# A list of doubtful rows cut in two blocks, expert blocks between and beside them, and one branch at the end of the tail

## The chip, the core and the metric

The kernel runs on one core of one Trainium2 chip. TensorE (PE) does the matrix products, VectorE (DVE) and ScalarE (ACT) the elementwise work and the copies out of PSUM, GpSimd (POOL) issues the indirect transfers (gathers and scatters of rows by index), SyncE (SP) the plain ones. The metric is the device time of one execution in microseconds (us), the median of several runs.

## The reference, cut to what matters

```python
x = _attn_ref(x, w_r, w_i, b_r, b_i).reshape(B * S, D)   # rfft, mix, shrink, irfft: 8 x 3072 rows of 256
h = x @ w_in                                             # first feed-forward, 2048 wide
x = (s * np.maximum(h, 0.0) ** 2 + b) @ w_out
logits = x @ w_gate                                      # second one: 8 experts of 1024, top 1
e = np.argmax(logits, axis=1)
gate = softmax(logits)[arange, e]
# a row is kept while its expert has had fewer than 768 rows before it, in order; out is 0 for the others
out[i] = gate[i] * (np.maximum(x[i] @ w1[e[i]], 0.0) @ w2[e[i]])
```

## The kernel before, in words

The order of the instructions is written out by hand (`manual_schedule`); each engine takes its own in that order. The main part (to about 1447 us) goes through the eight batches, 64 steps (`s_unit`) each. It finds for every row by a bound whether the row can go to an expert that isn't full. The first 1024 rows are computed exactly; after them one expert is full, and only rows whose choice stays open are put on a list in DRAM (`list`), at the place counted in `base` (one `decide_items` for each batch, whose last eight pieces are POOL scatters, L877).

`tail` does the rest:

- `decide_items` of the last batch, among `blocks[0]` and `blocks[1]`. A block (`block_steps`) is 128 rows of the full expert: two transposes (L1413), a copy `yT` by ACT, 32 matmuls `ph` (L1423), 16 matmuls `po` (L1433), the gated copy `o` by ACT and a scatter to `out` by POOL (L1438). There are `blocks[0]` to `blocks[5]`; each begins with transposes that wait for nothing but its rows and ends with matmuls into one PSUM tile.
- `whole_list`: a branch (L888) whose body writes the whole list anew where a lane had more than eight listed rows.
- `ids`: reads 512 entries of the list (an SP transfer `ci`, then eight small DVE operations), `load` gathers their rows (`ga`, two POOL gathers for 256 rows).
- `blocks[2]`, then `e2_steps` twice: for 256 listed rows each the exact logits and the exact output of the first feed-forward (`x_in`, L923; `x_mm`, L934; `x_out`, L949; `x_lg`, L957).
- `xroute_items` (softmax, ranks, tables `T`; DVE chains with four small matmul groups) among the ten steps of `blocks[3]`.
- `e2_more`: a branch (L1555) whose body takes more than two blocks of listed rows and then repeats the six blocks.
- `final_tables` (six pieces `a, d, e, d1, f, g`) among the twenty steps of `blocks[4]` and `blocks[5]`. The last piece `g` makes the indices of the other experts' rows and issues every load of theirs: gathers `yr`, `gg`, `nr`, `ng` and ten weight transfers of 1 MiB (`w`, `wb`, two `wq`, `wa`; each expert is a `w1`, L1348, and a `w2`, L1349).
- `item(0)`, nested with `item(1)`, ... (L1445): one block of another expert inside a branch each. `small(0)`, nested with `small(1)`, ... (L1463): up to three experts of at most 32 rows each, inside a branch.

A branch not taken is a jump over its body on every engine; behind it each engine makes up for the semaphore steps of the body, and POOL does so with `INC_SWDGE_SEM`.

Of the kernel before, what the change touches and what calls it, by code (L numbers as in the profile page):

```python
# [18 lines left out]
S = 3072  # L19
# [105 lines left out]
S_FROM = 27  # L125
S_TO = 62
# [22 lines left out]
class Kern:  # L149
# [625 lines left out]
    def route_consts(self, pp):  # L775
# [29 lines left out]
        self.cmax = zero("cmax", [1])  # L805
# [75 lines left out]
    def whole_list(self):  # L881

        nc, V = self.nc, self.nc.vector
        ovf = nc.values_load(self.ovf[0:1, 0:1], min_val=0, max_val=128)
# [355 lines left out]
    def final_tables(self, p2):  # L1240
# [30 lines left out]
        def e():  # L1271
# [12 lines left out]
            V.tensor_copy(out=t("ints", [2], I32), in_=endb[:, :, E - 1])  # L1284
# [158 lines left out]
    def item(self, n):  # L1443

        with self.tc.If(self.nblk > n):  # L1445
            if n > 1:
                self.load_item(n)
                self.rows(self.yr[n % 2], self.idy[:, n:n + 1])
                self.gate(n)
            for f in self.block_steps(self.wx[n % 2], self.yr[n % 2], self.gg[n % 2], self.ids[:, n:n + 1], "o2"):  # L1450
                f()
            if n + 1 < NI:
                self.item(n + 1)

# [4 lines left out]
    def small(self, g):  # L1459

        nc, pq = self.nc, self.pq
        P = 32 * NQ
        with self.tc.If(self.nsml > NQ * g):  # L1463
            if g:
                self.small_load(g, *range(NQ))
                self.rows(self.nr[:P], self.nids[:, 2, g:g + 1])
                self.gather(self.ng[:P], self.gd, self.nids[:, 0, g:g + 1])
            pt = pq.tile([128, 512], F32, tag="py", name="pt4", bufs=4)
            for h in range(2):
                nc.tensor.transpose(pt[:, h * P:(h + 1) * P], self.nr[:P, h * 128:(h + 1) * 128], self.ident[:P, :P])  # L1470
            yT = self.pb.tile([128, 2, P], F32, tag="yT", name="yT", bufs=2)
            nc.scalar.copy(out=yT.rearrange("p h c -> p (h c)"), in_=pt[:, :2 * P])
            hs, hT, os = {}, {}, {}

            def first(n):

                ps = pq.tile([128, 512], F32, tag="h", name="ph4", bufs=3)
                for h in range(2):
                    for j in range(4):
                        nc.tensor.matmul(ps[32 * j:32 * j + 32, :C], yT[:, h, 32 * n:32 * n + 32],  # L1480
                                         self.wq[n][0][:, h, C * j:C * (j + 1)], start=(h == 0), stop=(h == 1),
                                         skip_group_check=True)
                hs[n] = self.pb.tile([128, 2, 128], F32, tag="yT", name="hs", bufs=2)
                nc.scalar.activation(out=hs[n].rearrange("p c f -> p (c f)"), in_=ps[:, :C], func=AF.Relu)

            def turn(n):
                pt = pq.tile([128, 512], F32, tag="py", name="pt5", bufs=4)
                for c in range(2):
                    nc.tensor.transpose(pt[:, c * 128:(c + 1) * 128], hs[n][:, c], self.ident)
                hT[n] = self.pb.tile([128, 2, 4, 32], F32, tag="xq", name="hT", bufs=4)  # L1490
                nc.vector.tensor_copy(out=hT[n].rearrange("p c j t -> p (c j t)"), in_=pt[:, :C])

            def second(n):
                po = pq.tile([128, 512], F32, tag="py", name="po4", bufs=4)
                for c in range(2):
                    for j in range(4):
                        nc.tensor.matmul(po[32 * j:32 * j + 32, :C], hT[n][:, c, j], self.wq[n][1][:, 2 * j + c],
                                         start=(c == 0), stop=(c == 1), skip_group_check=True)
                os[n] = self.pb.tile([128, C], F32, tag=("eh", "el", "y")[n], name="os", bufs=(2, 2, 1)[n])
                nc.scalar.copy(out=os[n], in_=po[:, :C])  # L1500
            for n in range(NQ + 3):
                for f, k in ((first, 0), (turn, 1), (second, 3)):
                    if 0 <= n - k < NQ:
                        f(n - k)
            pr = pq.tile([128, 512], F32, tag="py", name="pr4", bufs=4)
            for n in range(NQ):
                nc.tensor.matmul(pr[32 * n:32 * n + 32, :C], self.sel, os[n], start=True, stop=True,
                                 skip_group_check=True)
            o = self.pb.tile([128, C], F32, tag="o4", name="o4", bufs=1)
            nc.scalar.activation(out=o[:P], in_=pr[:P, :C], func=AF.Copy, scale=self.ng[:P])  # L1510
            nc.gpsimd.indirect_dma_start(  # L1511
                out=self.out, out_offset=bass.IndirectOffsetOnAxis(ap=self.nids[:, 1, g:g + 1], axis=0),
                in_=o[:P], in_offset=None, bounds_check=self.B * S - 1, oob_is_err=False)
            if g + 1 < NS:
                self.small(g + 1)
# [29 lines left out]

    def e2_more(self, p2, again):
# [3 lines left out]
        bi, rem, blk = self.rt("e2i", [1], I32), self.rt("e2r", [1]), self.rt("e2b", [2])  # L1550
# [3 lines left out]
        n = nc.values_load(bi[0:1, 0:1], min_val=0, max_val=(self.B * S - XT) // TD)  # L1554
# [22 lines left out]
    def tail(self, es, e1, e3, p2):  # L1577
# [23 lines left out]
        tables, regs = self.final_tables(p2b)  # L1601
# [11 lines left out]
        def load(k):  # L1613
            x[k] = self.x_load(self.gbuf[k % 2], x["c"][3][:, 2 * k:2 * k + 2])
# [5 lines left out]
        self.lg_fin(B - 1, 7)  # L1620
        blocks = [block(j) for j in range(NJ)]
# [27 lines left out]
        among(blocks[4] + blocks[5], tables)  # L1649
        regs()  # L1650
        self.item(0)
        self.small(0)


    def run(self):
# [5 lines left out]
        with ExitStack() as es, tc.manual_schedule():  # L1661
# [89 lines left out]
            for b in range(B):  # L1751
# [15 lines left out]
                if b == B - 1:  # L1767
# [15 lines left out]
                    slot.setdefault(S_TO, []).extend(lambda j=j: self.full_rows(j) for j in range(NJ))  # L1783
                    self.yf = [p2.tile([128, C], F32, tag=f"yf{j}", name=f"yf{j}") for j in range(NJ)]
# [27 lines left out]
                for k in range(64):  # L1812
# [9 lines left out]
                    while fin and fin[0][0] <= 64 * b + k:  # L1822
                        _, fb, fi = fin.pop(0)
                        self.lg_fin(fb, fi)
                        if fi == 7 and fb > 1:
                            todo += self.decide_items(fb)
                    if todo:
# [53 lines left out]
```

## Time and profile before

| | us |
|---|---|
| median of 3 runs | 1633.86 |
| the three runs | 1641.65, 1633.6, 1633.86 |
| profiled execution, its own time | 1641.85 |
| its span, first to last instruction | 1640.1 |
| mean granted TensorE clock, share of full speed | 0.964 |

Times in the profile count from the first instruction of the span. "Idle before, releaser" tells how long an engine had nothing to do before an instruction and which instruction's end let it go on; "issue" is a wait that no recorded event explains. A jump has no busy time: it is seen as COMPARE_BRANCH on the sequencer (PEldq for PE). The clock column is the share of 2.4 GHz that was granted; 0.5 is 1.2 GHz.

### The profile page before, as it was taken

How to read it: one execution, taken by the hardware profiler on the slowest of the kernel's cores; microseconds unless marked ns; L12 is line 12 of the kernel's file. 1: busy time of each engine (PE TensorE's matmuls, PEld its weight loads, DVE VectorE, ACT ScalarE, POOL GpSimd, SP SyncE). 2: the span in 40 equal slices, each digit the busy share in tenths (PEclk: the TensorE clock that was granted, in tenths of full speed). 3: DMA queues.
4: the chain of work that ended last, by engine and by line, in shares of the span. 5: the costliest groups of instructions: out<-in, count | busy, mean ns of one | idle time of the engine just before them, and what ended most of it. 6: DMA issues, size and time to landing. Idle time of an engine off the chain costs nothing. (4 is left out here: it accounts for less than half of the span.)

```text
span 1640.1 us, 26008 instructions
## 1 busy us (share of the span) xinstructions
PE 1474.6 (90%) x9469; PEld 1223.8 (75%) x9469; DVE 957.3 (58%) x2057; ACT 814.6 (50%) x1252; POOL 267.8 (16%) x235
## 2 busy tenths in 40 slices
PE   8987899989998799999999999999999978988865
PEld 5876688777876578768877887787688768977753
DVE  2956467446555667656765775576567675623410
ACT  2335633754334564575467447645754665623311
POOL 0534100100000130030013002100300161231020
PEclk9998999999999899999999999999999989989978
DMA  8625644644434454464456446544644356510034
GB/s 258 219 91 187 170 141 145 188 128 128 144 111 139 113 145 138 144 165 139 130 148 169 144 125 171 152 137 144 165 142 128 97 136 204 170 40 17 14 113 174
DMA packets 273572, 230.03 MB, mean 140 GB/s; under 512 B 120045, under 2 KB 228335, under 8 KB 273424
## 3 DMA queue, kind: packets, MB, share of 16 engines
q1 hardware_dynamic: 255664, 200.13, 42.5%
q10 hardware_dynamic: 13936, 25.21, 4.1%
q0 software_dynamic: 3824, 2.82, 0.7%
q8 instruction: 80, 1.31, 0.4%
q14 instruction: 68, 0.56, 0.1%
HBM read 114.18 MB, written 114.09 MB: 139 GB/s over the span
## 5 line engine op out<-in xcount | busy, mean ns | idle before, releaser
L723 PE MATMUL ph<-ah,win 128*128 128x384 f32 (+1 forms) x2048 | 490.7, 368 | 7.4 <-ACT r L728 6.7
L728 ACT ACTIVATE r<-ph 128x768 bf16<-128x768 f32 (+1 forms) x512 | 396.0, 784 | 162.4 <-PE ph L723 118.8
L729 DVE TENSOR_TENSOR qb<-r 128x768 bf16<-128x768 bf16 (+1 forms) x512 | 300.8, 589 | 286.3 <-ACT r L728 258.7
L723 PEld LDWEIGHTS ph<-ah,win 128*128 128x128 f32 x2048 | 347.5, 194 | 77.6 <-issue 40.4
L333 PE MATMUL pmx<-wm,l 128*128 128x256 f32 x1196 | 297.1, 387 | 17.4 <-DVE kb L343 9.6
L396 POOL TENSOR_TENSOR asq<-ah 128x768 bf16<-128x768 f32 x64 | 96.2, 1504 | 1049.0 <-ACT ah L392 977.0
L333 PEld LDWEIGHTS pmx<-wm,l 128*128 128x128 f32 x1196 | 221.1, 191 | 54.7 <-DVE kb L343 16.0
L390 PEld LDWEIGHTS pi<-f1t,u 96*128 96x128 f32 x1024 | 131.3, 199 | 17.1 <-issue 8.4
L390 PE MATMUL pi<-f1t,u 96*128 96x96 f32 x1024 | 135.9, 284 | 6.1 <-DVE l L260 4.3
L224 PE MATMUL pz<-x,f 96*96 96x512 f32 x240 | 125.3, 606 | 3.7 <-DMA f<-c_f 3.7
L259 ACT COPY l<-pf 128x512 f32<-128x512 f32 x84 | 49.2, 586 | 144.5 <-PE pf L251 144.1
L371 ACT COPY v<-pi 128x512 f32<-128x512 f32 x96 | 56.3, 587 | 125.2 <-PE pi L369 125.2
L369 PE MATMUL pi<-t,e 128*128 128x256 f32 x384 | 99.5, 382 | 5.1 <-DVE t L328 5.1
L251 PEld LDWEIGHTS pf<-d,zp 128*128 128x128 f32 x672 | 89.5, 195 | 13.0 <-issue 7.9
L251 PE MATMUL pf<-d,zp 128*128 128x128 f32 x672 | 90.6, 279 | 8.2 <-DMA zp<-zd 8.2
L406 DVE STREAM_TRANSPOSE at<-pi 128x384 f32<-128x384 f32 x128 | 74.1, 579 | 34.1 <-ACT ah L392 25.5
L392 ACT CAST ah<-pi 128x384 fp32r<-128x384 f32 x128 | 61.1, 479 | 59.1 <-PE pi L390 58.9
L369 PEld LDWEIGHTS pi<-t,e 128*128 128x128 f32 x384 | 72.6, 191 | 17.5 <-DVE t L328 6.9
L232 ACT COPY z<-pz 96x512 f32<-96x512 f32 x120 | 69.8, 581 | 25.0 <-PE pz L224 18.3
L328 DVE TENSOR_TENSOR t<-t,cl 128x512 f32<-128x512 f32 x96 | 73.1, 762 | 3.3
L877 POOL DMA_INDIRECT list<-c,x x64 | 65.7, 1027 | 45.1 <-DVE c L873 29.0
L759 ACT COPY ls<-lg 128x384 f32<-128x384 f32 (+1 forms) x64 | 52.8, 825 | 24.0 <-PE lg L746 13.6
(395 smaller groups left out, 1818.6 us busy)
## 6 DMA issues: line engine op xcount, KB each, us to landing
zd<-z SPq DMA_DIRECT2D x128, 192.0 KB
zp<-zd SPq DMA_DIRECT2D x96, 256.0 KB
vd<-v ACTq DMA_DIRECT2D x96, 256.0 KB
u<-vd SPq DMA_DIRECT2D x64, 384.0 KB
ad<-at SPq DMA_DIRECT2D x256, 96.0 KB
out<-zero SPq DMA_DIRECT2D x96, 256.0 KB
x<-x SPq DMA_DIRECT2D x120, 192.0 KB
sd<-stage SPq DMA_DIRECT2D x32, 256.0 KB
```

The source lines that it names most:

```text
L224: nc.tensor.matmul(o, self.f1, xs.rearrange("p a c -> p (a c)"), start=True, stop=True)
L232: nc.scalar.copy(out=z.rearrange("p a c -> p (a c)"), in_=o)
L251: nc.tensor.matmul(pv[:, h, :, gi * 64:gi * 64 + 64], zp[:, gi, h * 128:(h + 1) * 128], self.d[:, 2 * p + gi, :].rearrange("p (t m) -> p t ...
L328: nc.vector.tensor_tensor(out=t, in0=t, in1=cl, op=ALU.subtract)
L333: self.nc.tensor.matmul(o, part(h), w[:, h], start=start and h == 0, stop=stop and h == 1, skip_group_check=True)
L369: nc.tensor.matmul(ps[:, gi * C:(gi + 1) * C], self.e[:, 2 * p + gi], t[:, gi * C:(gi + 1) * C], start=True, stop=True)
L390: nc.tensor.matmul(ps[:, :TC].rearrange("p (a n) -> p a n", n=4)[:, :, n], u[:, n, h::2], self.f1t, start=True, stop=True)
L396: nc.gpsimd.tensor_tensor(out=self.asq[b, i], in0=af, in1=af, op=ALU.mult)
L406: nc.vector.transpose(out=self.ar[:, :, :, h], in_=self.at.pop((b, i, h))[:, :TC].rearrange("p (g c) -> p g c", c=32))
L723: nc.tensor.matmul(ps[:, j, :n], self.win[:, k, f], ah[:, k, t0:], start=(k == 0), stop=(k == 1))
L728: nc.scalar.activation(out=r, in_=ps[:, :, :n], func=AF.Relu)
L729: nc.vector.tensor_tensor(out=q, in0=r, in1=r, op=ALU.mult)
```

## The change: what it does

1. **First list block early.** At step 60 of the last batch `first_block` reads the first 256 list entries, copies `base` to `early` and gathers their rows. In the tail the first `e2` block (`part(0)`) takes the place of `blocks[0]` and `blocks[1]` as the work among which the last batch is decided.
2. **`whole_list`** is also taken where `early` is under 256, and its body ends with `redo`: `part(0)` again with a fresh read and gather.
3. **Between the list blocks**: `ids`, one gather of 256 rows, then `blocks[0]` and `blocks[1]`, then the second `e2` block. `line` writes two blocks so that the second one's transposes stand before the first one's `po` matmuls.
4. **Beside the ranks**: `xroute_items` among the twenty steps of `blocks[2]` and `blocks[3]`. The number for the second branch is computed (`e2_number`) and read into registers (`e2_count`) before them.
5. **Beside the tables**: all six pieces stand among the first ten steps of `line(blocks[4:])`, so `g` comes after the `po` matmuls of `blocks[4]`; ten steps follow it.
6. **One branch**: the steps of items 0 and 1 (in `line`) and of the first group of small experts (`small_do(0)`) always run. One number, `more`, is read at the end; the branch holds `item(2)` and `small(1)` with their own nests.

The diff (unchanged lines of `small` that only lost a level are left out):

```diff
@@ whole_list
+    def whole_list(self, redo):
+        V.tensor_scalar(out=self.early, in0=self.early, scalar1=float(TD), scalar2=None, op0=ALU.is_lt)
+        V.tensor_tensor(out=self.ovf, in0=self.ovf, in1=self.early, op=ALU.add)
+        ovf = nc.values_load(self.ovf[0:1, 0:1], min_val=0, max_val=129)
...
                 for n in range(N2):
                     self.to_list(n, x, c)
+            redo()
@@ final_tables
+            more = t("more", [2])
+            for k, n in enumerate((2, NQ)):
+                V.tensor_scalar(out=more[:, k:k + 1], in0=endb[:, k, E - 1:E], scalar1=float(-n), scalar2=0.0, op0=ALU.add, op1=ALU.max)
+            V.tensor_tensor(out=v["ints"][:, 2:3], in0=more[:, 0:1], in1=more[:, 1:2], op=ALU.add)
...
         def r():
             ints = v["ints"]
-            self.nblk = nc.values_load(ints[0:1, 0:1], min_val=0, max_val=NI)
-            self.nsml = nc.values_load(ints[0:1, 1:2], min_val=0, max_val=E - 1)
+            more = nc.values_load(ints[0:1, 2:3], min_val=0, max_val=NI + E)
+            with self.tc.If(more > 0):
+                self.nblk = nc.values_load(ints[0:1, 0:1], min_val=0, max_val=NI)
+                self.nsml = nc.values_load(ints[0:1, 1:2], min_val=0, max_val=E - 1)
+                self.item(2)
+                self.small(1)
@@ e2
+    def e2_count(self):
+        self.nlist = self.nc.values_load(self.bi[0:1, 0:1], min_val=0, max_val=(self.B * S - XT) // TD)
+
+    def first_block(self):
+        c = self.e2_ids(2, self.list[0:TD], None, self.base)
+        self.nc.vector.tensor_copy(out=self.early, in_=self.base)
+        self.first_rows = self.x_load(self.gbuf[0], c[3])
@@ tail
-        blocks = [block(j) for j in range(NJ)]
-        among(blocks[0] + blocks[1], self.decide_items(B - 1))
-        self.whole_list()
+        def part(k, rows):
+            return self.e2_steps(lambda: rows, lg, 2 * k, self.yx[XT + TD * k:XT + TD * (k + 1)])
+
+        def redo():
+            c = self.e2_ids(2, self.list[0:TD], None, self.base)
+            for f in part(0, self.x_load(self.gbuf[0], c[3])):
+                f()
+
+        def line(blocks):
+            it = [f for f in blocks[0][:5]]
+            for n, b in enumerate(blocks):
+                nx = blocks[n + 1] if n + 1 < len(blocks) else []
+                it += nx[:1] + b[5:] + nx[1:5]
+            return it
+        blocks = [block(j) for j in range(NJ)]
+        among(part(0, self.first_rows), self.decide_items(B - 1))
+        self.whole_list(redo)
         ids()
-        for k in range(min(SB, 2)):
-            load(k)
-        lg = self.rt("e2g", [2 * SB, E])
-        for f in blocks[2]:
+        rows = self.x_load(self.gbuf[1], x["c"][3][:, 2:4])
+        self.e2_number()
+        for f in line(blocks[0:2]) + part(1, rows):
             f()
-        for k in range(SB):
-            st = self.e2_steps(lambda k=k: x[k], lg, 2 * k, self.yx[XT + TD * k:XT + TD * (k + 1)])
-            st.pop(0)()
-            if k + 2 < SB:
-                load(k + 2)
-            for f in st:
-                f()
+        self.e2_count()
...
-        among(blocks[3], side)
+        among(line(blocks[2:4]), side)
...
-        among(blocks[4] + blocks[5], tables)
-        regs()
-        self.item(0)
-        self.small(0)
+        it = line(blocks[4:])
+        among(it[:10], tables)
+        for f in it[10:]:
+            f()
+        for f in line([self.item_steps(n) for n in range(2)]):
+            f()
+        self.small_do(0)
+        further()
@@ run
+                    slot.setdefault(LIST_AT, []).append(self.first_block)
```

## Rows read from the trace of the kernel before

**Rows 1.** The page: span, and TensorE's clock in 40 slices of it.

```profile
span 1640.1 us, 26008 instructions
...
PEclk9998999999999899999999999999999989989978
```

**Rows 2.** Stretches of the tail: length; busy PE, PEld, DVE, ACT, POOL; clock; DMA, GB/s.

```profile
1449.30:1457.00 7.70, 6.22 (x28) 5.83 (x29) 3.58 (x12) 0.97 (x2) 4.73 (x5) 0.56 0.32 102
...
1515.95:1545.99 30.04, 28.17 (x233) 24.65 (x231) 12.29 (x20) 10.30 (x18) 0.00 (x0) 1.00 0.03 10
1563.99:1569.60 5.61, 5.09 (x23) 4.69 (x23) 1.12 (x8) 0.92 (x2) 0.00 (x0) 0.50 0.01 3
...
1617.10:1629.30 12.20, 9.74 (x110) 4.49 (x110) 1.27 (x3) 3.05 (x8) 0.94 (x1) 0.85 0.06 21
1629.30:1640.10 10.80, 0.00 (x0) 0.00 (x0) 0.00 (x0) 0.00 (x0) 0.00 (x0) 0.58 0.03 7
```

**Rows 3.** Waits of PE from 1440 us on: who waited for whom.

```profile
PE pt L1413 <- DMA yr<-zd,idi: 7.9, 1, 7.9
PE pt L1470 <- ACTq L1445: 6.4, 1, 6.4
PE pt L1413 <- DVE sc L1283: 5.8, 1, 5.8
PE ph L1423 <- ACT yT L1415: 3.9, 7, 0.7
PE ptb L1117 <- DVE ol L1110: 2.4, 2, 2.0
PE pt L923 <- DMA ga<-ad,cw: 2.1, 2, 1.3
PE ph L1423 <- issue: 2.1, 1, 2.1
...
PE pt L1413 <- PEq L888: 1.3, 1, 1.3
```

**Rows 4.** PE's jump at each branch line: duration ns min/median/max, first, last start.

```profile
L888 PEldq COMPARE_BRANCH  x1: 247/247/247, 1467.5 to 1467.5; - x1
...
L1555 PEldq COMPARE_BRANCH  x1: 3914/3914/3914, 1559.5 to 1559.5; - x1
...
L1445 PEldq COMPARE_BRANCH  x1: 6357/6357/6357, 1608.0 to 1608.0; - x1
...
L1463 PEldq COMPARE_BRANCH  x3: 65/197/3648, 1614.8 to 1630.8; - x3
```

**Rows 5.** Timeline of PE: the end of the last batch, one block.

```profile
1448.65 0.64 PE L767 MATMUL plt<-ident,ls 128*96 128x128 f32 x4 [0.91 <-ACT ls L759]
...
1603.46 3.84 PE L1423 MATMUL ph<-yT,wb 128*128 128x128 f32 x32 [0.66 <-ACT yT L1415]
1607.14 3.62 PE L1433 MATMUL po<-wb,h 128*128 128x256 f32 x16
```

**Rows 6.** Timeline of SP: the weight transfers' issue, first and last.

```profile
1585.73 0.40 SPq L1348 DMA_DIRECT2D w<-moe_w  x1
...
1602.05 5.59 SPq L1348 DMA_DIRECT2D wa<-moe_w  x1
```

**Rows 7.** Stretches of the weight transfers, columns as in rows 2.

```profile
1585.73:1617.60 31.87, 17.45 (x102) 15.40 (x102) 0.00 (x0) 3.97 (x8) 8.02 (x8) 0.78 1.00 347
...
1617.60:1620.30 2.70, 2.24 (x22) 0.97 (x24) 0.00 (x0) 0.40 (x2) 0.00 (x0) 0.50 0.14 49
```

**Rows 8.** Timeline of all engines: the third small expert, the last scatter.

```profile
1621.68 1.07 PE L1480 MATMUL ph<-wa,yT 128*32 128x256 f32 x16
...
1628.32 0.94 POOL L1511 DMA_INDIRECT out<-o,idn  x1 [15.45 <-ACTq L1463]
```

**Rows 9.** Timeline of SP and POOL: reading the list, gathering its rows.

```profile
1477.59 0.38 SPq L1523 DMA_DIRECT2D ci<-list  x1
...
1480.83 1.04 POOL L1395 DMA_INDIRECT ga<-ad,cw  x1 [6.37 <-DVE e2p L1611]
```

More of the change, by code (lines that the diff above doesn't have):

```diff
@@ L125 @@
 S_FROM = 27
+LIST_AT = 60
 S_TO = 62
@@ L1283, in e @@
             V.tensor_tensor(out=sc[:, 0:2], in0=endb, in1=sc[:, 2:4], op=ALU.subtract)
-            V.tensor_copy(out=t("ints", [2], I32), in_=endb[:, :, E - 1])
+            V.tensor_copy(out=t("ints", [3], I32)[:, 0:2], in_=endb[:, :, E - 1])
+            more = t("more", [2])
+            for k, n in enumerate((2, NQ)):
+                V.tensor_scalar(out=more[:, k:k + 1], in0=endb[:, k, E - 1:E], scalar1=float(-n), scalar2=0.0, op0=ALU.add, op1=ALU.max)
+            V.tensor_tensor(out=v["ints"][:, 2:3], in0=more[:, 0:1], in1=more[:, 1:2], op=ALU.add)
         def f():
@@ L1445, in item @@
         with self.tc.If(self.nblk > n):
[L1446 to L1450, printed above, removed]
+            self.load_item(n)
+            self.rows(self.yr[n % 2], self.idy[:, n:n + 1])
+            self.gate(n)
+            for f in self.item_steps(n):
                 f()
@@ L1453, in item, with item_steps @@
                 self.item(n + 1)
+    def item_steps(self, n):
+        return self.block_steps(self.wx[n % 2], self.yr[n % 2], self.gg[n % 2], self.ids[:, n:n + 1], "o2")
     def small_load(self, g, *qs):
@@ L1459, in small, with small_do @@
     def small(self, g):
+        P = 32 * NQ
+        with self.tc.If(self.nsml > NQ * g):
+            self.small_load(g, *range(NQ))
+            self.rows(self.nr[:P], self.nids[:, 2, g:g + 1])
+            self.gather(self.ng[:P], self.gd, self.nids[:, 0, g:g + 1])
+            self.small_do(g)
+            if g + 1 < NS:
+                self.small(g + 1)
+    def small_do(self, g):
         nc, pq = self.nc, self.pq
         P = 32 * NQ
[L1463 to L1468, printed above, removed]
-            for h in range(2):
[L1470 to L1515, printed above, removed]
@@ new lines, in small_do, with first @@
+        pt = pq.tile([128, 512], F32, tag="py", name="pt4", bufs=4)
+        for h in range(2):
+            nc.tensor.transpose(pt[:, h * P:(h + 1) * P], self.nr[:P, h * 128:(h + 1) * 128], self.ident[:P, :P])
+        yT = self.pb.tile([128, 2, P], F32, tag="yT", name="yT", bufs=2)
+        nc.scalar.copy(out=yT.rearrange("p h c -> p (h c)"), in_=pt[:, :2 * P])
+        hs, hT, os = {}, {}, {}
+        def first(n):
+            ps = pq.tile([128, 512], F32, tag="h", name="ph4", bufs=3)
+            for h in range(2):
+                for j in range(4):
+                    nc.tensor.matmul(ps[32 * j:32 * j + 32, :C], yT[:, h, 32 * n:32 * n + 32],
+                                     self.wq[n][0][:, h, C * j:C * (j + 1)], start=(h == 0), stop=(h == 1),
+                                     skip_group_check=True)
+            hs[n] = self.pb.tile([128, 2, 128], F32, tag="yT", name="hs", bufs=2)
+            nc.scalar.activation(out=hs[n].rearrange("p c f -> p (c f)"), in_=ps[:, :C], func=AF.Relu)
@@ new lines, in turn, with second @@
+        def turn(n):
+            pt = pq.tile([128, 512], F32, tag="py", name="pt5", bufs=4)
+            for c in range(2):
+                nc.tensor.transpose(pt[:, c * 128:(c + 1) * 128], hs[n][:, c], self.ident)
+            hT[n] = self.pb.tile([128, 2, 4, 32], F32, tag="xq", name="hT", bufs=4)
+            nc.vector.tensor_copy(out=hT[n].rearrange("p c j t -> p (c j t)"), in_=pt[:, :C])
+        def second(n):
+            po = pq.tile([128, 512], F32, tag="py", name="po4", bufs=4)
+            for c in range(2):
+                for j in range(4):
+                    nc.tensor.matmul(po[32 * j:32 * j + 32, :C], hT[n][:, c, j], self.wq[n][1][:, 2 * j + c],
+                                     start=(c == 0), stop=(c == 1), skip_group_check=True)
+            os[n] = self.pb.tile([128, C], F32, tag=("eh", "el", "y")[n], name="os", bufs=(2, 2, 1)[n])
+            nc.scalar.copy(out=os[n], in_=po[:, :C])
@@ new lines, in small_do @@
+        for n in range(NQ + 3):
+            for f, k in ((first, 0), (turn, 1), (second, 3)):
+                if 0 <= n - k < NQ:
+                    f(n - k)
+        pr = pq.tile([128, 512], F32, tag="py", name="pr4", bufs=4)
+        for n in range(NQ):
+            nc.tensor.matmul(pr[32 * n:32 * n + 32, :C], self.sel, os[n], start=True, stop=True,
+                             skip_group_check=True)
+        o = self.pb.tile([128, C], F32, tag="o4", name="o4", bufs=1)
+        nc.scalar.activation(out=o[:P], in_=pr[:P, :C], func=AF.Copy, scale=self.ng[:P])
@@ L1518, in e2_ids @@
+        nc.gpsimd.indirect_dma_start(
+            out=self.out, out_offset=bass.IndirectOffsetOnAxis(ap=self.nids[:, 1, g:g + 1], axis=0),
+            in_=o[:P], in_offset=None, bounds_check=self.B * S - 1, oob_is_err=False)
     def e2_ids(self, M, src, start, rem):
@@ L1553, in e2_more @@
         V.tensor_scalar(out=bi, in0=bi, scalar1=8, scalar2=None, op0=ALU.arith_shift_right)
-        n = nc.values_load(bi[0:1, 0:1], min_val=0, max_val=(self.B * S - XT) // TD)
+        self.bi = bi
+    def e2_count(self):
[4 more added lines that the diff above has]
+        self.first_rows = self.x_load(self.gbuf[0], c[3])
+    def e2_more(self, p2, again):
+        nc, tc, V = self.nc, self.tc, self.nc.vector
+        rem, blk = self.rt("e2r", [1]), self.rt("e2b", [2])
+        n = self.nlist
         with tc.If(n > SB):
@@ L1600, in tail @@
         self.nr, self.ng = t("nr", [C]), t("ng", [1])
-        tables, regs = self.final_tables(p2b)
+        tables, further = self.final_tables(p2b)
         w0 = self.wx[0]
@@ L1826, in run @@
                             todo += self.decide_items(fb)
+                    assert b < B - 1 or k < LIST_AT or not todo
                     if todo:
```

13 lines of the change are left out of this document (5 added, 8 removed).

## Prediction

> **What bounds the kernel now.** The page first: its clock line stands at 9 or 10 tenths in nearly every slice and falls at the end [rows 1]; there, in the tail, PE stops and comes back at half clock. The change touches only the tail and two lines of step 60, so the next view is who PE waits for from 1440 us on [rows 3]. The reader is to see three waits that make up 20 us of the 32 listed: 7.9 for the first rows of the other experts, 6.4 behind the branch of the items, 5.8 behind the branch for more list blocks (the engine named there, DVE, is not the cause: PE's own jump is). Then the jumps themselves [rows 4]: PE needs 0.25 us for the skip at L888, 3.91 at L1555, 6.36 at L1445, 3.65 at L1463. Then stretches at either clock [rows 2]: a list block runs 30.0 us at full clock; behind the 5.8 us wait the first 5.6 us run at 0.50. Last the weight transfers [rows 6, 7]: from the first issue at 1585.73 the DMA engines are full (share 1.00, 347 GB/s) until 1617.6, and nearly empty after 1620.3. That is a bound of its own, since ten transfers of 1 MiB are needed before the last small expert can be finished.
>
> **The change, walked along PE**, in the time of the profiled execution, with rows 5 for a block's parts (ph 3.84, po 3.62, wait for yT 0.66; with the transposes some 8.3).
>
> *Start.* The last logits are transposed by 1448.65 + 0.64 = 1449.3 [rows 5]. The first list block can begin at once: its read of the list is queued on SP ahead of the store of step 61, and the two gathers go through POOL before those of the six blocks' rows. From the list's read to the first gather took 1477.59 to 1480.83 [rows 9]; I cost it at nothing, since the PE products of steps 60 to 63 run meanwhile and need nothing of it. If SP came late to the read, DVE would stand still behind it and the squares of a step with it: up to those 3.2, once. The block: 30.0 [rows 2] + 3.4 for the clock (6.8 of the first 7.7 us were granted half, mean 0.56 [rows 2], as the end of the last batch leaves PE waiting either way) + 0.3 for the small products of the decision. The eight list scatters follow in POOL's queue with nothing else queued between. End: **1483.0**.
>
> *First branch.* Before, it cost 1.3 + 2.1 [rows 3]. Now two DVE operations stand ahead of it and its body grows: from 16 matmuls with 16 weight loads to 230 with 230 (the redo is a list block: 64 x 3 and 16 + 16 matmuls and some transposes). What the larger skip costs no row shows. Bounds: 0.25 as before, and 6.36, the longest [rows 4]. The nearest row is L1463, where 236 instructions (two groups of 59 matmuls and loads) are passed over in 3.65, and L1555, 3.91 for some thousand; I take 3.9. With the DVE operations and the register read ahead of it, the whole wait is that of L1555, 5.8 [rows 3]. POOL waits there too, for its transfers and its semaphore step; behind it are the gathers of the second list block, 18 us ahead of their use. End: **1488.8**.
>
> The Trainium skill (Runtime: NRT & Kernel Launch, Instruction fetch mechanics) says that a taken branch whose target lies outside the fetched pages stalls for a fetch, and gives PE's instruction memory as 2048 instructions. By that size a skip of 460 would stay inside, and the sum be that of the short skip below, 1611; L1463's 3.65 for 236 speaks against it.
>
> *Blocks 0 and 1.* Two blocks less one wait for yT: 2 x 8.3 - 0.66 = 16.0, + 2.8 for half clock after the wait (5.6 us at 0.50 [rows 2]). End **1507.6**. The list read and the gather for the second block lie under them: some 6 us from the list's read to the first use (3.2 to the gather [rows 9], some 3 for it to land), behind POOL's step.
>
> *Second list block*, without the 2.1 wait for its rows: 30.0, **1537.6**. *Blocks 2 and 3 with the ranks*: 16.0 + 1.0 for the rank products; the 2.4 that PE waited for DVE [rows 3] go, as there is a block more to cover the DVE chains. **1554.6**.
>
> *Second branch.* The number is in registers long before. PE's sequencer runs ahead of the array (at L1445 it began the jump at 1608.0 [rows 4], while the po matmuls ran to 1607.14 + 3.62 = 1610.76 [rows 5]), so of 3.91 some 1.2 show, with the restart 2.0. Bounds: nothing and the old 5.8. **1556.6**, against 1563.99 [rows 2]: 7.4 gained.
>
> *Tables.* From there to the first weight issue took 1585.73 - 1563.99 = 21.7 [rows 2, 6]. Now one ph, one po and one wait for yT (8.1) come after the loads instead of before: 13.6, first issue at **1570.2**. The gathers `yr` keep their 7.9 [rows 3], and that block work covers them.
>
> *Items and small experts.* PE alone would need 8.1 for the block, 16.7 for both items, and for the small ones 12.2 - 0.9 at a clock of 0.85 [rows 2], 11 or a little less: the last scatter some 35.7 after the first issue. The transfers need more: the ninth MiB (the third small expert's first half) lands 1617.6 - 1585.7 = 31.9 after the first issue [rows 7], and from that expert's first matmul to the last scatter took 1628.32 - 1621.68 = 6.6 [rows 8]. I add 1.2 for a PE that has waited and runs at half clock for part of it: 39.7. End: **1609.9**, where before it was 1628.3: 18.4 gained. The 6.4 behind the items' branch thus go, but a new wait of about 4, for the weights, takes part of their place. Loads queue on SP as before; its own waits (5.59 at the last [rows 6]) come from the full queue, not from the kernel.
>
> *End.* The skip at the end remains (L1463's 3.65 ran beside POOL's work), with a register read added: 0.5. The 10.8 behind the last POOL scatter [rows 2] stay.
>
> Sum: 18.4 - 0.5 = 17.9, so 1641.85 - 17.9 = 1624 for an execution like the profiled one. That one is 8 us above the median of the three runs, one of which is like it; the median is nearer to the usual, so the forecast is 1633.86 - 17.9 = **1616**.
>
> **The rivals.**
>
> *The weights are no bound, or the first skip is short.* PE alone ends 4 earlier (39.7 to 35.7): 1612. A skip of 0.25 saves 3.7 and about 1.1 of clock: 1611. With both, 1607. For it: the mean of 347 GB/s holds a slow start, and L888's own skip was short. Against: the share of 1.00 over the whole stretch [rows 7], and L1463's row. Chance 0.2.
>
> *The skips cost their full price.* The first takes 6.4, as under full DMA, the second shows its whole 5.8 and its half clock, and the start of the second list block waits some for POOL: 2.5 + 3.8 + 1.1 = 7.4 more, 1623. For it: the joins wait for the slowest engine (the 6.4 are put down to ACT [rows 3]). Chance 0.2.
>
> *The redo is taken* (the other side). If the list holds under 256 entries at step 60, the body runs: a list read, a gather, 6 us, and a list block, 30 us, none of it covered, less the skip of 3.9: 1616 + 32 = 1648, slower. It decides at 256 entries. The trace does not show the count; that the branch for more than two blocks was skipped shows at most 512 in all. Worked out from the reference's inputs with the kernel's bound, 420 to 450 stand there after seven batches, and at most 494 in all. Chance 0.05.
>
> *No change that can be measured.* The loads move up only if nothing holds them; if SP came to them late (held by the wait for a buffer in `win` and `wl`, or POOL by its semaphore step), the first issue stays where it is and what remains is the 7.4 ahead of the tables: 1627. Chance 0.05.
>
> **How the numbers follow.** My forecast has 0.5. The measurement can tell about 0.5%, 8 us, from no change. Faster by more: the forecast and its two neighbours, 0.9. Within 8 us: 0.05. Slower: 0.05. Range: the low end 1606, a short skip and no bound by the weights; the high end 1627, full skips with 4 us more for a slower transfer, or no earlier loads. An execution like the profiled one (1624) lies inside.
>
> **What the profile would show.** PE's first list block at about 1449, no `yf` wait; a skip at the first branch of about 3.9 on PE and an idle PE of 5 to 6 us; no wait for `ga` or `ol`; about 2 us at the second branch; the first weight issue about 15 us earlier; a wait of `ph<-wa` for its transfer in the small experts, 3 to 5 us; nothing between items and small experts. Wrong would be: `redo` running; DVE or POOL held in the last steps of the batch by the list's read; a wait at `pt<-ga` of the second list block; weights landing at another pace.

## The result, and the profile after

The changed kernel took 1614.69 us (median of 4, 1614.46 to 1615.16) where the kernel before took 1634.83 on the same chip (1633.6 to 1641.65): a ratio of 0.9869, 95% interval 0.9841 to 0.9897. The forecast was 1616. On two other chips the same pair gave 0.9929 [0.9904, 0.9953] and 0.9925 [0.9907, 0.9944]; the gain is between 11 and 20 us, and the end of this document comes back to that spread. One execution of the kernel with the late tables, below, took 1655 us at a granted clock of 0.918 where its others had 0.962 to 0.969; it is left out.

The page of the profiled execution (1614.86 us), against [rows 1]:

```profile
span 1612.6 us, 25987 instructions
...
PEclk9997999999999899999999999999999999999997
```

In the tail the clock line now falls only in its last slice, and the span is 27.5 us shorter. Not all of that is the change. The tail starts when the last logits are transposed (L767 before, L768 after). It lasted 190.8 us before and 173.2 now, 17.6 less; the other 10 arose ahead of it. About half of them is one wait of 5.4 us for a product of batch 7 (`ya`) in that execution of the kernel before, which the change doesn't touch; the rest stays open. So all that follows is measured along the tail.

Stretches of the tail after, cut at the steps of the prediction (the first begins 0.2 us early, with the list block's own transposes); columns as in [rows 2]:

```profile
1439.20:1471.95 32.75, 30.22 (x234) 26.28 (x232) 15.38 (x36) 10.40 (x18) 13.34 (x13) 0.95 0.09 25
1471.95:1477.54 5.59, 0.01 (x2) 0.04 (x1) 0.93 (x4) 0.00 (x0) 0.00 (x0) 0.78 0.16 54
1477.54:1494.57 17.03, 16.57 (x101) 15.36 (x102) 1.35 (x11) 3.50 (x7) 3.06 (x3) 0.87 0.10 25
1494.57:1524.79 30.22, 28.29 (x232) 24.77 (x231) 11.42 (x18) 10.76 (x19) 1.01 (x1) 1.00 0.01 5
1524.79:1540.72 15.93, 15.47 (x108) 13.87 (x106) 8.87 (x47) 5.17 (x10) 0.98 (x1) 1.00 0.08 26
1540.72:1545.93 5.21, 0.01 (x2) 0.04 (x1) 4.28 (x28) 0.31 (x1) 0.98 (x1) 0.75 0.10 35
1545.93:1559.07 13.14, 12.62 (x91) 11.16 (x92) 1.69 (x12) 2.77 (x6) 0.00 (x0) 0.84 0.01 1
1559.07:1580.49 21.42, 20.82 (x141) 19.12 (x140) 0.00 (x0) 5.05 (x10) 8.03 (x8) 1.00 0.99 341
1580.49:1590.90 10.41, 4.09 (x49) 1.95 (x51) 0.42 (x1) 1.45 (x4) 1.97 (x2) 0.85 1.05 376
1590.90:1598.28 7.38, 6.53 (x66) 2.66 (x58) 0.85 (x2) 1.97 (x5) 0.00 (x0) 0.75 0.08 25
1598.28:1612.60 14.32, 0.00 (x0) 0.00 (x0) 0.00 (x0) 0.00 (x0) 0.94 (x1) 0.61 0.03 8
```

In order: list block 1, the first skip, blocks 0 and 1, list block 2, blocks 2 and 3 with the ranks, the second skip, the work up to the first weight issue, blocks and items under the weights, the first small experts (PE busy for 4.09 of 10.41 while the DMA engines are full), the rest of them, and the end from the last scatter on. Who PE waits for from 1430 us on, against [rows 3]:

```profile
PE pt L1427 <- PEq L892: 5.6, 1, 5.6
PE pt L1427 <- DVE ints L1293: 5.2, 1, 5.2
PE ph L1501 <- SPq L1346: 4.4, 1, 4.4
PE ph L1437 <- ACT yT L1429: 2.0, 4, 0.6
...
PE ph L1501 <- DMA wq<-moe_w: 1.1, 1, 1.1
```

The 7.9 for `yr`, the 6.4 at the items' branch and the 2.1 for `ga` are gone from the list. There are two skips of over 5 us, and a new wait of 4.4 for the weights of the third small expert (`ph<-wa`; the view names SP's branch). The instructions at the branch lines show what the skips consist of, against [rows 4]:

```profile
L892 PEldq COMPARE_BRANCH  x1: 3667/3667/3667, 1473.6 to 1473.6; - x1
...
L892 POOLq INC_SWDGE_SEM  x1: 1820/1820/1820, 1477.2 to 1477.2; - x1
...
L1588 PEldq EVENT_SEMAPHORE  x2: 51/51/51, 1543.3 to 1543.5; - x2
...
L1588 PEldq COMPARE_BRANCH  x1: 3559/3559/3559, 1539.7 to 1539.7; - x1
...
L1588 POOLq COMPARE_BRANCH  x1: 58/58/58, 1541.1 to 1541.1; - x1
L1588 POOLq INC_SWDGE_SEM  x1: 1910/1910/1910, 1543.8 to 1543.8; - x1
...
L1346 POOLq EVENT_SEMAPHORE  x5: 17/43/43, 1601.1 to 1601.4; - x5
...
L1346 POOLq COMPARE_BRANCH  x1: 45/45/45, 1598.4 to 1598.4; - x1
L1346 POOLq INC_SWDGE_SEM  x1: 2131/2131/2131, 1601.5 to 1601.5; - x1
```

At L1588 PE's jump is over at 1543.3, but PE starts again only at 1545.93, just after POOL's INC_SWDGE_SEM ends (1543.8 + 1.91 = 1545.7). POOL had issued the scatter of block 3 right at the branch, and it took 2.4 us to land:

```profile
1541.30 0.98 POOL L1452 DMA_INDIRECT out<-o,f_id  x1 [6.25 <-ACTq L1588]
...
DMA to landing us min/median/max: 2.4/2.4/2.4
```

So the step begins as that scatter lands (1541.3 + 2.4 = 1543.7), and it decides there, as the experiments show. At L892 it doesn't: PE starts at 1477.54, while the same step of POOL runs from 1477.2 to 1479.0.

### The profile page after: what moved, and what is told of

Read it like the earlier page. It is cut to its first block, busy times and chain, and to the rows that moved or that the text cites. A ratio compares the mean times of both kernels' runs of the same rounds, so it can differ in the third digit from the quotient of the medians.

```text
span 1612.6 us, 25987 instructions
## 1 busy us (share of the span) xinstructions
PE 1467.8 (91%) x9469; PEld 1218.9 (76%) x9469; DVE 958.6 (59%) x2071; ACT 814.9 (51%) x1252; POOL 269.4 (17%) x235
## 5 line engine op out<-in xcount | busy, mean ns | idle before, releaser
L334 PEld LDWEIGHTS pmx<-wm,l 128*128 128x128 f32 x1196 | 221.2, 191 | 53.2 <-DVE kb L344 15.9
L407 DVE STREAM_TRANSPOSE at<-pi 128x384 f32<-128x384 f32 x128 | 74.1, 579 | 38.4 <-ACT ah L393 30.1
L878 POOL DMA_INDIRECT list<-c,x x64 | 66.7, 1043 | 56.3 <-DVE c L874 40.6
L760 ACT COPY ls<-lg 128x384 f32<-128x384 f32 (+1 forms) x64 | 53.2, 831 | 18.6 <-PE lg L747 16.8
```

Of the source, the lines that this page charges most:

```text
L334: self.nc.tensor.matmul(o, part(h), w[:, h], start=start and h == 0, stop=stop and h == 1, skip_group_check=True)
L407: nc.vector.transpose(out=self.ar[:, :, :, h], in_=self.at.pop((b, i, h))[:, :TC].rearrange("p (g c) -> p g c", c=32))
```

## The experiments

Twelve runs followed: ten more kernels, and the changed kernel twice again. The first group (the items' branch, the tables late, the lists, the third expert's weights) shared a chip on which the kernel before took 1640.8 us and the changed kernel was not run; the second had one with 1634.97, the third one with 1637.94. "Tail" is the time from the last logits' transposes to the end of the span, in the one profiled execution of each.

### The control

> The changed kernel once more, as the control beside the three kernels that follow and beside the four experiments of the first group, whose chip gave other times for the kernel before (1640.8 against 1634.8 us). If the stages of the tail belong to the kernel, its tail (from the end of the last decision of batch 7) is again 173.2 us long, within 1.5, with waits of 5.6 and 5.2 us at the two skips, and no more than 39.2 + 0.7 us from the first weight issue to the last scatter. If the tail is longer in general on another chip, the 182.3, 183.8 and 181.2 us of the three kernels that took a part of the change back are worth as much less.

> The changed kernel a third time, as the control beside the three kernels that follow. From its two earlier profiled executions: a tail of 172.8 to 173.2 us, waits of 5.6 to 5.7 and of 5.20 at the two skips, first weight issue 119.7 to 120.0 after the tail's start, 38.4 to 39.2 from there to the last scatter, 14.3 to the end; 0.987 to 0.993 of the kernel before.

Measured: 1621.77 us (0.9929 of before) and 1627.04 (0.9925). Tails 172.8 and 174.1, waits at the skips 5.7 and 5.20 in both, first weight issue 120.0 and 120.1 after the tail's start, from there to the last scatter 38.4 and 39.6. The tail belongs to the kernel, to within some 1.3 us; what differs more between executions is when it starts (1439.4, 1442.6 and 1449.8 us). Two points of the tail serve below as rulers: PE starts again behind the second skip 106.6, 105.3 and 106.6 us after the tail's start, and from there to the end of the span it is 66.7, 67.5 and 67.5.

### The items' branch back

```diff
-        for f in line([self.item_steps(n) for n in range(2)]):
-            f()
-        self.small_do(0)
         further()
+        self.item(0)
+        self.small(0)
...
```

With it the number `more` is no longer read, and the numbers for the nested branches are read in its place.

> The items and the first group of small experts stand in their nested branches again, as before the change; all else as after the change. Theory (from the first weight issue on, the transfers of 10 MiB set the end): the skip of some 6 us behind the items only takes the place of the wait for the last weights (4.4 us for wa, 1.1 for wq), so 0 to 2 us more: 1615 to 1617. Rival (the removed branch was itself worth its wait): 6.4 us more, 1621.

Measured: 1631.34 us, 0.9933 [0.9914, 0.9952] of before, which is not apart from the changed kernel's 0.9929 and 0.9925 on the other chips; the tail tells more. It is 182.3, 9 longer than with the change, but half of that is not this edit's: PE came out of the second skip 4.4 us late, after longer waits in the first list block (2.6 and 1.5 for DVE's `xq`, where the changed kernel waits at most 1.1 at a time). From the second skip to the end it is 71.3, 4 to 4.6 longer. PE's waits:

```profile
PE pt L1489 <- ACTq L1455: 5.6, 1, 5.6
...
PE ph L1433 <- issue: 3.5, 1, 3.5
```

The skip over the third item (PE's jump took 6.19 us there) costs its 5.6 in full and isn't hidden behind the weights, for with it the wait for the third small expert is gone (it had landed by then), and yet the last scatter comes 6.5 to 7.2 us later behind the second skip; the end behind it is 2.6 shorter (11.7 against 14.3). The 3.5 is PE's wait for the `yT` of item 0, which stood on ACT behind the `o` of block 5, and that waited 5.3 us for a releaser that the view calls "remote". In a run of the changed kernel the same wait was 1.8, so only a part of it can be this edit's. My theory (0 to 2 us more) falls, and the rival's 6.4 is too much: about 4.

### The tables late

```diff
-        among(it[:10], tables)
-        for f in it[10:]:
-            f()
+        among(it, tables)
```

> Only the place of the tables is undone: the six pieces are spread over all twenty steps of blocks 4 and 5, so every load of the other experts is issued about 8 us later. Theory (the end hangs on the first weight issue): the whole 8 us come back, 1622 to 1623, with the wait for wa unchanged at about 4. Rival (the loads were covered anyway, the branch was the gain): 1615 to 1616.

Measured: 1636.41 us (median of nine), 0.9961 [0.9938, 0.9985]; tail 183.8, first weight issue at +130.0 instead of +120, and PE waits 7.0 for `yr` again ([rows 3]: 7.9). Of the 10 us about 3 are again the first list block's (the 2.6 for `xq`; PE out of the second skip at +109.5). From the second skip to the end it is 74.3, 7 to 7.6 longer, near the theory's 8: ten steps behind the tables move the weight stream by that, and they cover the gathers.

### The lists in the old place

The first list block goes back behind the first branch, `redo` out of that branch's body, and the read of the second branch's number behind the ranks:

```diff
-        among(part(0, self.first_rows), self.decide_items(B - 1))
+        among(blocks[0] + blocks[1], self.decide_items(B - 1))
         self.whole_list(redo)
...
+        for k in range(2):
+            x[k] = self.x_load(self.gbuf[k], x["c"][3][:, 2 * k:2 * k + 2])
+        for f in blocks[2]:
...
-        among(line(blocks[2:4]), side)
+        among(blocks[3], side)
```

> The list part is undone: blocks 0 and 1 beside the last decision, list read and gathered late, both list blocks behind each other, the ranks beside one block, the number for the second branch read at the branch, no first block at step 60 and no redo in the first branch's body; tables, items and end as after the change. Theory (the two halves of the gain are independent, 8.0 us of it ahead of the tables): 1622 to 1623. Rival (the loads at the end absorb what comes earlier or later ahead of them): 1615 to 1617.

Measured: 1634.28 us, 0.9943 [0.9913, 0.9973]; tail 181.2, 7 to 8 longer, of which 5 to 6 ahead of the second skip's end. The first skip is cheap again (PE's jump 0.24), but waits of 2.1 and 2.7 follow it that the view doesn't assign, then 2.0 for `ol`, and 5.4 for the second skip. The three parts undone one by one, measured where each edit acts, cost some 4, 7 and 8, together about the 17.6 of the whole: that their gains overlap is not shown.

### Without the third small expert's weights

```diff
-        self.wq.append(cut(wa))
+        self.wq.append(self.wq[0])
...
-            self.small_load(0, *range(NQ))
+            self.small_load(0, *range(NQ - 1))
```

The third small expert is computed with the first one's weights, and two transfers of 1 MiB are left out.

> Leaves out two of the ten weight transfers: the third small expert computes with the first one's weights. Theory (the transfers set the end): the wait of 4.4 us for wa goes and some 0.8 us of half clock behind it, 1609 to 1610.5; the first two small experts may still wait 1 us. Rival (PE or the queue of scatters sets the end): 1614 to 1615.

Measured: 1622.19 us, 0.9874 [0.9845, 0.9902]; from the first weight issue to the last scatter 34.2 instead of 39.2 (38.4 and 39.6 in the other two runs), no wait for weights. The tail is only 1.8 shorter, 171.4, since this execution too had the 2.6 for `xq` in the first list block. The transfers do bound that stretch, by the 4 us that the prediction gave (39.7 - 35.7) and a little more.

### A short first skip

```diff
-            redo()
```

> The redo of the eight router passes is left out of the body of the first never-taken branch, so that the first skip jumps over the list's loop alone. Theory: the length of TensorE's jump goes with what is jumped over; its first jump falls from 3.67 to about 0.25 us, as it was in the kernel before (0.25), the wait there from 5.6 to about 2.1, and the time by 3.5, to about 1611. Rival A: the 5.6 us are set by GpSimd's and ScalarE's end of the same skip, or by the number that the branch is waiting for; then the jump is short and the wait stays over 4.5, the time within 1 us. Rival B: a jump's length doesn't go with what it skips; then the jump stays at 3.6. As a by-product the code behind the second skip moves by the length of the redo; if its 5.2 us change by 2, the position of the code behind the jump matters.

Measured: 1617.88 us, 0.9894 [0.9874, 0.9914]; PE's jump and the wait:

```profile
L892 PEldq COMPARE_BRANCH  x1: 228/228/228, 1477.5 to 1477.5; - x1
```

```profile
PE pt L1425 <- DVE pk L1296: 5.4, 1, 5.4
PE ph L1499 <- DMA wa<-moe_w: 4.2, 1, 4.2
...
PE pt L1425 <- PEq L892: 2.0, 1, 2.0
```

The theory holds for this skip: 0.23 us for 16 matmuls with their loads, 3.67 for those and the redo's 230, and the wait falls from 5.7 on this chip to 2.0. But the length doesn't grow with what is jumped over: 236 instructions cost 3.65 [rows 4], these 492 cost 3.67, and some thousand 3.4 to 3.9. It is a step, and the view of the DMA queues, cut to the time of each jump, shows what it consists of: in every one of the 40 PE jumps of over 3 us in the tails of all fourteen traces there is one transfer of 16 KiB on the instruction queue (q8), and in none of the 14 shorter ones. A long jump holds a fetch of instructions.

Of the 3.7, 2.4 are left at the first weight issue (+117.6). The tail is no shorter all the same (172.6 against 172.8): from the issue to the last scatter it took 40.5 instead of 38.4. From the second skip to the last scatter PE has the same 339 matmuls in both; it was busy with them for 45.99 us here and 44.71 in the run without this edit, at mean clocks of 0.84 and 0.87, and waited 0.7 longer. So busy time took 1.3 of the 2.4 back, and the waits 0.7. Why the clock was lower, no run told apart.

### Shifted code

One line more in the body of `e2_more`'s branch, with 128 in the second kernel:

```diff
+            self.warm(64)
```

> 64 never-run matmuls more in the body of the second branch (128 TensorE instructions, 8 KiB of code), nothing else. Theory: of the 5.2 us at the second skip about 2.2 come from a second fetch of TensorE's instructions just behind the jump's target (16 KiB that came 1.2 us after the jump), because the end of a fetched piece lies there; with the code shifted by half a piece the second fetch falls elsewhere, and the wait falls to about 3.0, the time by 2.2, to 1612.5. Rival: the 5.2 us are one wait for the branch's number and the jump, whatever the position; then nothing changes (within 0.5 us).

> The same with 128 never-run matmuls (256 TensorE instructions, 16 KiB, just one fetched piece). Theory: the code behind the target lies in its piece as without them, so the wait is 5.2 us again, and the time that of the changed kernel. Rival: what counts is not the place in a piece but how far the jump goes; then the wait grows with the jump, or falls in both kernels alike.

Measured: 1619.18 and 1619.26 us (0.990 both), and the wait at the second skip is 5.20 us in both, as without. The fetch of instructions behind the jump, which I had taken for its cause, isn't. What stays the same to 0.01 us when the code is moved is no question of where the code lies; of the other engines' steps at L1588, POOL's, shown above, fits. The two tails are 172.5 and 175.7: with nothing changed that runs, the same 339 matmuls behind the second skip kept PE busy for 44.9 and 46.2 us. A difference of 1 or 2 us in one tail is therefore no effect by itself.

### Nothing in flight at the second skip

```diff
+            def put():
+                nc.gpsimd.indirect_dma_start(
...
+            if tag == "o2":
+                put()
+            else:
+                self.put = put
...
+        blocks = [block(j, "o3" if j == 3 else "o2") for j in range(NJ)]
...
         self.e2_more(p2, again)
+        self.put()
```

> Block 3's rows are written to the output behind the second skip instead of ahead of it, nothing else (in the redone case, which this data doesn't take, they would be written from the first pass). Theory, formed when shifted code left the 5.20 us as they were: at the skip GpSimd waits until every scatter it issued has landed (that of block 3, issued as the branch came, landed 2.5 us later), then spends 1.91 us on adding up the queues' semaphores, and TensorE's first instruction behind the skip waits for one of these, whatever line the view of waits names. With nothing in flight GpSimd is through before TensorE's own jump is over; the wait falls from 5.2 to 3.0 (what is left of the jump of 3.5), the first weight issue comes no later, and the tail is up to 2.2 shorter. Rival: it is VectorE's chain that the view of waits names, from the ranks' sum to the count of items; then the wait stays 5.2 us, since that chain isn't touched.

Measured: 1621.12 us, 0.9903 [0.9876, 0.9929]. The branch's instructions and the waits:

```profile
L1593 POOLq COMPARE_BRANCH  x1: 58/58/58, 1538.8 to 1538.8; - x1
...
L1593 POOLq INC_SWDGE_SEM  x1: 1890/1890/1890, 1541.5 to 1541.5; - x1
L1593 PEldq COMPARE_BRANCH  x1: 3652/3652/3652, 1544.7 to 1544.7; - x1
```

```profile
PE pt L1427 <- PEq L892: 5.5, 1, 5.5
PE ph L1506 <- SPq L1346: 4.4, 1, 4.4
PE pt L1427 <- DVE idw L1267: 3.2, 1, 3.2
```

The theory holds in the main: POOL is through before PE jumps (1541.5 + 1.89 = 1543.4), and the wait falls from 5.2 to 3.2, which is PE's own jump. Something was in flight even so: POOL issued the scatter of block 2 at the branch, at 1539.0, and its step began 2.5 us later, at 1541.5; only this now lay under PE's work. The view of waits still names DVE, and now another instruction of it, whichever had just ended. The tail is 173.0, 1.1 shorter than the changed kernel's on that chip, which is within what differs anyway: that the 2 us reach the end is not shown.

### The tables sooner, and all three

```diff
-        among(it[:10], tables)
-        for f in it[10:]:
+        among(it[:3], tables)
+        for f in it[3:]:
```

> The six table pieces stand among the first three steps of blocks 4 and 5 instead of the first ten. Theory: they are done some 7 us earlier, and with them the first weight issue (from +119.8 to about +113); the weights then land 7 us earlier by the clock, the 4.4 us wait for the third small expert goes, and TensorE is the bound from there: no more than 5.0 of the 7 are won (without that expert's transfer the way from the first issue to the last scatter was 34.2 instead of 39.2), so 4.5 to 5.5 off the tail. Rival: the pieces hold the blocks' own VectorE or ScalarE work up, or the earlier weights meet the blocks' transfers and land no earlier; then less than 2.

Measured: 1615.97 us, 0.9866 [0.9845, 0.9886], where the changed kernel on that chip had 0.9925 [0.9907, 0.9944]: 11 us less by the medians, 6.8 of them in the tail (167.3), more than the theory's 5.5. The first weight issue comes at +114.8, 5.3 earlier, and no wait for weights is left. From the second skip to the last scatter 46.4 us remain of 53.2. Of these 6.8, 4.9 are waits, the 4.4 for the weights above all. The other 1.9 are clock: PE was busy with the same 339 matmuls for 42.6 us instead of 44.5, since without that wait it keeps full speed through the small experts, where the rows after had 0.85 and 0.75:

```profile
1561.10:1589.30 28.20, 26.65 (x176) 24.25 (x175) 0.00 (x0) 6.40 (x13) 9.03 (x9) 1.00 1.00 350
1589.30:1599.30 10.00, 8.26 (x111) 4.00 (x109) 1.27 (x3) 3.42 (x9) 1.00 (x2) 1.00 0.44 151
```

The last kernel has the scatter's edit, the tables' edit, and the first branch's number read four steps earlier:

```diff
+        first = part(0, self.first_rows)
+        among(first[:-4], self.decide_items(B - 1))
+        self.whole_number()
+        for f in first[-4:]:
+            f()
```

> Three edits at once: block 3's scatter behind the second skip, the tables among the first three steps, and the first branch's number worked out and read four steps ahead of the end of the first list block instead of behind it (the first wait then about 2 instead of 5.6 us, since the jump starts under TensorE's work). If what is won ahead of the first weight issue is kept: 3.6 + 2.2 + 5 = 10.8 off the tail, 162 us, and some 1604 where the changed kernel takes 1614.7. Rival: the weights' stream bounds the end whatever comes ahead of it, but the stream's own start follows the tables, so a loss would show as a wait for the third small expert of over 2 us; then 6 to 8 off.

Measured: 1613.81 us, 0.9852 [0.983, 0.9874], the lowest median of the study on its chip, 13 below the changed kernel there, but not apart from the tables alone (0.9866 [0.9845, 0.9886]); and the tail is 167.0, only 0.3 below theirs, where 162 was hoped for. Its waits up to the first skip:

```profile
PE lg L966 <- DVE xq L986: 2.4, 3, 1.2
PE pt L1431 <- PEq L896: 1.9, 1, 1.9
PE ph L943 <- DVE ovf L885: 1.5, 1, 1.5
PE prt L864 <- DVE t L859: 1.5, 1, 1.5
```

The first skip did fall to 1.9, but it begins 5.4 us later. The waits for DVE ahead of it are longer, which fits the decision's DVE work pressed among fewer steps, and the number itself (`ovf`) holds a step up. So PE comes out of this skip 1.9 us later than with the tables alone. From there on the clock counts for more than the waits. Behind the short first skip it was full:

```profile
1483.70:1500.70 17.00, 15.77 (x105) 14.32 (x105) 1.78 (x12) 4.56 (x9) 3.90 (x4) 1.00 0.11 31
```

The second skip fell to 2.9, and PE comes out of it at +103.4, 3.2 earlier than with the tables alone. Behind it the granted clock was 0.51 over the 9.2 us to the first weight issue (0.67 over 8.2 with the tables alone), and the 339 matmuls kept PE busy for 46.0 us instead of 42.6. That gives the gain back, and neither theory had it.

## Why the prediction was right, step by step

Each step in us, the prediction's end minus its start against the rows after:

| step | predicted | measured |
|---|---|---|
| first list block | 33.7 | 32.8 |
| first skip | 5.8 | 5.6 |
| blocks 0 and 1 | 18.8 | 17.0 |
| second list block | 30.0 | 30.2 |
| blocks 2 and 3, ranks | 17.0 | 15.9 |
| second skip | 2.0 | 5.2 |
| to the first weight issue | 13.6 | 13.1 |
| first issue to last scatter | 39.7 | 39.2 |
| last scatter to the end | 12.3 | 14.3 |
| sum | 172.9 | 173.4 |

**Right.** That the two list blocks run at their old 30 us, the first with half clock at its start; that the first skip takes the longer jump of its larger body, 3.67 where 3.9 was taken from the nearest row; that the first weight issue comes some 13 us after the second skip; that the gathers `yr` are covered; that the weight stream becomes the bound, with a wait of about 4 (measured 4.4). The short-skip experiment shows the second of these, the kernel without the third expert's weights the last.

**The Trainium skill's size.** The Trainium skill (Runtime: NRT & Kernel Launch, Instruction fetch mechanics) gives PE's instruction memory as 2048 instructions, and by that size the prediction had a short first skip as the rival. The trace disagrees: the skip cost PE 3.67 us. (The body has 492 instructions, not 460, as the loop's own 32 come on top of the redo's; without the redo the jump took 0.23.) The Trainium skill also says there that a taken branch to a target outside the fetched pages stalls for a fetch. The trace agrees: each long jump has its transfer on the instruction queue. One price for all larger bodies is also why 3.9 from the nearest row came close.

**Mis-sized, and cancelling.** The second skip was put at 2.0 and took 5.2. The step was "so of 3.91 some 1.2 show, with the restart 2.0": it looked at PE's sequencer alone. PE's jump did begin under its own work, 1.0 ahead of the array's end. But POOL waited there for the scatter of block 3, issued at the branch, and then took 1.91 for its semaphores. In the kernel before, the reading was right: PE's jump at L1555 ended at 1563.4 [rows 4], after POOL's step at 1562.5; the change brought the branch up against a scatter. The lines of before that this rests on, and that of its end:

```profile
L1555 POOLq INC_SWDGE_SEM  x1: 1910/1910/1910, 1560.6 to 1560.6; - x1
...
L1463 POOLq INC_SWDGE_SEM  x1: 2123/2123/2123, 1628.5 to 1628.5; - x1
```

The rival "the skips cost their full price" had this ("the joins wait for the slowest engine"), though not the engine. The end was put at 12.3 and took 14.3. The step that failed is "a register read added: 0.5". POOL's own step isn't what was added, as it took 2.12 there before and takes 2.13 now. But before it began 0.2 us after the last scatter was issued (1628.32), and now 3.2 after it: POOL is at the branch at 1598.4 and at its first step behind it at 1601.1. What holds POOL for these 2.7 us no view names; with the nested branches back, the end was 11.7. Against these 5.2 stand 3.8 of too much for half clock and for the ranks in the first five steps. The next two steps were 0.9 too long as well. The sum is right to 0.5 partly by that luck.

**What the clock cost.** I gave the first list block 6.8 us at half clock, as before [rows 2]; it had 3.4, so the whole stretch shows 0.95. Behind the first skip the granted clock was 0.87 over 17 us, not 0.5 for the first 5.6 and more.

**What stays open.** The tail accounts for 17.6 us, 1.1%. The medians differ by 20, 13 and 11 on three chips, so that the first one came within 2 us of 1616 is in part luck too; for an execution like the profiled one the prediction had 1624, and it took 1614.86. Ahead of the tail the two kernels share all but the early list read at step 60; whether that costs some microseconds on the two later chips no run tells, as the start of the tail moves by 10 us between executions of one kernel. The kernel with the lists in the old place, without that read, started its tail at 1451.7, among the 1447.0 to 1453.4 of the other three on that chip, which is no sign of it. Why three kernels on that chip waited 2.6 us in the first list block, which none of their edits touches, stays open. Not tried: a second skip with neither a scatter in flight nor a long jump.

## What to carry to other kernels

A skipped branch is priced by the slowest engine of it, so list all of them. For PE it is the jump, some 3.6 us with a fetch of instructions in it and 0.2 without. For POOL it was, at the second skip, the landing of the scatter issued just before plus its own 1.9 us. Keep indirect transfers away from a branch, and rarely needed bodies small: here 32 instructions were cheap and 236 were not. When a stream of transfers is the bound, the cheapest gain is its start: the steps that release it belong first, with work left over to cover what follows; but pressing one engine's side work among fewer steps can hold the main work up. And compare PE's busy time for the same matmuls: where a shorter wait is followed by a lower granted clock, 2 or 3 us won can be gone again before the end.

## What the runs showed that was not expected

- POOL's INC_SWDGE_SEM at a join took 1.8 to 2.1 us at each of these branches. At the second skip it began only as the scatter issued just before had landed (1543.7 and 1543.8); at the last branch of the kernel before it did not wait for that (issue 1628.32, step 1628.5). The view of waits doesn't name it: it named DVE's `ints`, `pk`, `idw`, in turn.
- PE's jump took 0.23 us for 32 instructions and 3.3 to 4.0 at the first two skips with larger bodies, 128 or 256 instructions more in them or not. Each long jump has one transfer of 16 KiB on the instruction queue, which starts 0.9 to 1.5 us after the jump does. At the items' branch, with the DMA engines full, the jump took 6.19 and 6.36 (before), and that transfer started only 3.7 and 3.8 us after it: the extra 2.7 us lie ahead of the transfer.
- A wait costs more than itself: with no wait for weights (tables sooner) the small experts ran at 1.00 instead of 0.75 to 0.85, and 1.9 us came back beside the wait. The same 339 matmuls took PE 42.6 to 46.2 us in the runs of the second and third group.
